# Attention's PSUM: four single slots chosen by an estimate in place of two rings of two, and the key load placed ahead of the maxima rows' loads

## The chip, the cores and the metric

The kernel runs on one core of one Trainium2 chip. The metric is the device time of one execution in microseconds (us). Before the change the median of 3 runs is 1422.26 us (1418.68 to 1423.93).

## The reference

For 8 batches of 8 heads, 1152 keys and 64 dimensions, neighbouring pairs of query rows are averaged to 576 queries, and softmax attention is computed with its row maxima subtracted. The result, as x of 576 x 512 for each batch, goes through a second part.

```
q_pool = q.reshape(B, H, S // 2, 2, D).mean(axis=3)
scores = scale * q_pool @ k^T;  scores -= max(scores);  attn = exp(scores)
x      = (attn / sum(attn)) @ v              # then heads side by side: 576 x 512
theta  = x @ w_theta;  y = w_tok_r @ (x cos theta) + w_tok_i @ (x sin theta)
u      = x + y;        out = u + max(u @ w_ch, 0)
```

## The kernel before, in words

The work is in two stages with a PSUM pool each. The first, attention, is what the change touches; the second (theta, token mixing, channel product) is left alone.

**The tiling of attention.** Heads go in 32 pairs i = 0 .. 31, the two heads side by side in the 128 partitions of the matrix array. A pair has two halves of 288 queries (u = 0, 1) with nine key tiles each (kt = 0 .. 8). For each (u, kt):

- `escore` (lines 354 to 374) makes the scores in eight matmuls, two heads by four terms: high by high part, high by low, low by high, and last the row of negated maxima (`nmr`, line 371). They go to a double bank `pe` of PSUM, from which ScalarE takes the exponential into a tile `pc` (line 374).
- `ssum` (376 to 383) adds the `pc` tiles on GpSimd to `ss`, 4.5 steps later.

The maxima of a pair are found one to two pairs earlier. `maxpass` (296 to 315) makes twelve rough score products, two matmuls each into a double bank `pm` (305), and VectorE reduces each (312). `max_tail` does the remaining 64 queries (`px`, `py`, lines 322 and 328), `max_nm` joins them (337), `max_row` transposes the result into `pmt` (342) and ScalarE copies it to `mT` (344). `load_max` then spreads `mT` into the row `nmr` with four DMAs (351, 352).

At two places of each pair a `burst` (456 to 466) comes between the score tiles.

- With u = 0: `prep_t` transposes queries and the last three key tiles of pair i + 2 into `pt` (265), which ScalarE copies to `hi` (281) and VectorE subtracts to `lo` (292); then `max_row` of pair i + 1; then `av`, 36 matmuls of `pc` by v into `pa` (392), copied out by ScalarE (399); then `norm_sum` of pair i - 1, twelve matmuls with ones (408), read by ScalarE (417). Before the change `norm_sum` writes the second bank of the tile `pmt` that `max_row` took.
- With u = 1: `prep_t` transposes the first six key tiles of pair i + 3, then `max_tail` of pair i + 2, then `av`.

So between two runs of `av` there is a **stretch** of nine score products `pe` with six maxima products `pm` among them. The order is the same in both halves: pe pm pe pm pe pm pe pe pm pe pm pe pm pe pe, and then the burst's transposes into `pt`.

**The order of the work.** Nothing is scheduled by a planner. Each step has a position written by hand (`at(position, priority, step)`), in units of one score tile; pair i begins at 18 i. The list is sorted by position, and each engine takes its instructions in that order. So an instruction that waits holds up all that is behind it on its engine. In between, at nine positions per pair (`W_AT`), a generator `weights` does one step of narrowing and splitting a tile of the second stage's weights, on VectorE (lines 525 to 540), ScalarE and GpSimd; it also takes a double bank (`pwt`, line 585) ten times in all.

**PSUM before.** Attention owns all eight banks as four double banks, made by `bank2` (148). Two form the ring "e": `pe` and `pa` (for pair 0 also two thirds of `pm`). Two form the ring "m": `pm`, `pt`, `px`, `py`, `pmt`, `pwt`. In a ring of two a use waits until the readers of the use before last in that ring are done.

**The queue of loads.** SyncE issues all DMAs of this stage in order. The key tile `kn` has one buffer: the load of pair i + 3 (line 226, two DMAs) has to wait for the last transposes of pair i + 2's keys, in the burst with u = 0. `PLAN` puts that load at 36 - 43.2 = -7.2 relative to the next pair's start, behind `load_max` at -7.6.

Of the kernel before, what the change touches and what calls it, by code (L numbers as in the profile page):

```python
# [9 lines left out]
F32 = mybir.dt.float32  # L10
# [21 lines left out]
    "load_q": -44.55,  # L32
    "load_k": -43.2,
    "pool_q": -35.35,
# [12 lines left out]
BANKS = {}  # L47
PAIRS = {"e": 2, "m": 2}
BANKS2 = {"h": 1, "t": 1, "m": 4, "r": 2}
# [42 lines left out]
def pooled_attention_moe_kernel(  # L92
# [12 lines left out]
    P = 128  # L105
# [10 lines left out]
    NPAIR = B * NP  # L116
# [8 lines left out]
    psum = {}  # L125
# [18 lines left out]
    def bank(kind, name):  # L144
        pool, bufs = psum["now"]
        return pool.tile([P, 512], F32, tag=kind, name=name, bufs=bufs[kind])

    def bank2(kind, name):
        return psum["now"][0].tile([P, 2, 512], F32, tag=kind, name=name, bufs=PAIRS[kind])

# [37 lines left out]
    with ExitStack() as p1:  # L188
# [63 lines left out]
        def prep_t(i, g):  # L252
            st = state[i]
            kn = st["kn"]
            pt = st["pt", g] = bank2("m", f"pt{g}_{i}")
            if g == 0:
                srcs = [[kn[:, t] for t in range(3 * n, 3 * n + 3)] for n in range(2)]
            else:
                qp = st["qp"]
                srcs = [[qp[:, t] for t in range(5)], [qp[:, 5]] + [kn[:, t] for t in (6, 7, 8)]]  # L260
            for n in range(2):
                c = 0
                for src in srcs[n]:
                    R = src.shape[0]
                    nc.tensor.transpose(  # L265
                        out=pt[:, n, c : c + R],
                        in_=src.rearrange("p h d -> p (h d)"),
                        identity=ident[0:R, 0:R],
                    )
                    c += R  # L270
# [25 lines left out]
        def maxpass(i):  # L296
# [4 lines left out]
            for j in range(4):  # L301
                for g in range(3):
                    pm = bank2("em"[g % 2] if i == 0 else "m", f"pm{i}_{j}{g}")
                    for h, hs in enumerate(HEADS):
# [12 lines left out]
        def max_tail(i, pt):  # L317
            st = state[i]
            hi, tl, mx = st["hi"], st["tail"], st["mx"]
            pm = bank2("m", f"px{i}")  # L320
            for n, c, k, w in ((0, 0, 0, 4), (1, 0, 4, 2), (1, 2 * P, 6, 2)):
# [4 lines left out]
            if pt is None:  # L326
                pt = bank2("m", f"py{i}")
            nc.tensor.matmul(
# [10 lines left out]
        def max_row(i):  # L339
            st = state[i]  # L340
            px = bank2("m", f"pmt{i}")
            nc.tensor.transpose(out=px[0:KT, 0, 0:P], in_=st["nm"], identity=ident)
            mT = st["mT"] = sml.tile([KT, P], F32R, tag="mT", name=f"mT{i}")
            nc.scalar.copy(mT, px[0:KT, 0, 0:P])
            return px

# [38 lines left out]
        def av(i, u):  # L385
            st = state[i]
            if u == 0:
                st["xu"] = nrm.tile([P, 2, HALF], F32, tag="xu", name=f"xu{i}", bufs=3)
            pa = bank2("e", f"pa{i}_{u}")
            for kt in range(KT):  # L390
# [65 lines left out]
        def burst(i, u):  # L456
            if u == 0:
                if i + 2 < NPAIR:
                    prep_all(i + 2, 1)
                px = max_row(i + 1) if i + 1 < NPAIR else bank2("m", f"pmt{i}")  # L460
                av(i, u)
                if i > 0:
                    norm_sum(i - 1, px)
            else:
                tail_prep(i)
                av(i, u)
# [29 lines left out]
        def weights():  # L496
# [78 lines left out]
            def token(wv, kb, jt):  # L575
# [8 lines left out]
                yield  # L584
                pw2 = bank2("m", "pwt")
                pt = pw2[:, 0]
# [55 lines left out]
        NU = 2 * KT  # L642
        todo = []

        def at(pos, prio, fn, *args):
            todo.append((pos, prio, len(todo), fn, args))
# [37 lines left out]
        for i in range(NPAIR):  # L684
            plan(i)
        at(NU * NPAIR + 2, 9, lambda: norm_sum(NPAIR - 1, bank2("m", "pend")))
        pw = ExitStack()
# [303 lines left out]
```

## Time and profile before

| what | value |
|---|---|
| median of 3 runs | 1422.26 us (1418.68 to 1423.93) |
| span of the profiled execution, first to last instruction | 1414.8 us |
| median of the runs less that span | 7.5 us |
| PE matmul busy | 1352.8 us, 96% |
| VectorE (DVE) busy | 862.2 us, 61% |
| ScalarE (ACT) busy | 730.6 us, 52% |
| GpSimd (POOL) busy | 911.4 us, 64% |
| chain that ended last: PE, DVE, ACT, DMA | 67%, 15%, 10%, 3% |

The profiled execution's own time is known only as its span; launch and end around the instructions lie outside it, so the median of the runs stands 7.5 us above it. Matmuls are pipelined: one of 288 columns is recorded as 0.29 us long though the next one starts 0.07 us later. The busy share of PE therefore hides short waits, and starts of instructions tell more than durations. A name such as `PE pe L371` is engine, tile written and line; "x2" in a row joins two instructions in a line.

### The profile page before, as it was taken

The numbers are of one execution on the slowest core, as the hardware profiler recorded it, in microseconds if no ns is written. First come the engines' busy times: TensorE is split into PE (matmuls) and PEld (weight loads), VectorE is DVE, ScalarE is ACT, GpSimd is POOL, SyncE is SP. The second block draws the span as 40 slices with busy tenths as digits, with TensorE's granted clock in tenths as the row PEclk, the third lists the DMA queues.
The fourth block names the chain that finished last, engine by engine and source line by source line (L and its number), as shares of the span: only waits on it lengthen the run. The fifth ranks groups of instructions, "written<-read, shape, count | busy, mean of one in ns | idle before, by whom it ended". The sixth has DMA issues, their size and how long they took to land.

```text
span 1414.8 us, 29922 instructions
## 1 busy us (share of the span) xinstructions
PE 1352.8 (96%) x12178; PEld 1086.1 (77%) x12178; DVE 862.2 (61%) x1143; ACT 730.6 (52%) x1250; POOL 911.4 (64%) x672
## 2 busy tenths in 40 slices
PE   5999999999999999999999999999999999999998
PEld 4667676766676767767776766688999999999998
DVE  5866676777577767766687666355362553536442
ACT  2556465655555655556565655465444544445431
POOL 2789888978798889889898888834232413232210
PEclk7999999999999999999999999999999999999999
DMA  5224343434342443324343421231111211111111
GB/s 127 74 75 126 85 111 84 119 85 116 86 125 69 108 122 106 94 83 125 84 111 86 119 80 51 79 122 38 35 38 34 60 50 34 38 35 44 28 31 38
DMA packets 130906, 111.66 MB, mean 79 GB/s; under 512 B 95040, under 2 KB 95424, under 8 KB 130768
## 3 DMA queue, kind: packets, MB, share of 16 engines
q1 hardware_dynamic: 130592, 109.28, 28.0%
q8 instruction: 96, 1.57, 0.5%
q0 software_dynamic: 176, 0.46, 0.1%
q14 instruction: 42, 0.34, 0.1%
HBM read 88.29 MB, written 21.27 MB: 77 GB/s over the span
## 4 chain that ended last, share of the span: by engine, by line
PE 67%; DVE 15%; ACT 10%; DMA 3%; issue 3%; POOL 1%; SPq 0%; ACTq 0%; POOLq 0%; DVEq 0%
PE pa L392 16%; PE pe L371 16%; PE py L821 11%; PE pth L743 7%; PE pr L860 5%; DVE mx L312 5%; ACT pc L374 4%; PE pm L305 3%; PE pt L265 3%; PE pmt L408 2%; DMA kn<-in_k_dram 2%; DVE wf L532 1%; PE pxn L731 1%; DVE ws L530 1%; DVE lo L292 1%
## 5 line engine op out<-in xcount | busy, mean ns | idle before, releaser
L383 POOL TENSOR_TENSOR ss<-ss,pc 128x576 f32<-128x576 f32 x384 | 558.1, 1453 | 98.2 <-ACT pc L374 75.9
L312 DVE TENSOR_REDUCE mx<-pm 128x2 f32<-128x768 f32 x384 | 343.9, 950 | 134.8 <-PE pm L305 134.4
L374 ACT ACTIVATE pc<-pe 128x576 f32<-128x576 f32 x576 | 371.2, 652 | 102.2 <-PE pe L371 84.2
L392 PE MATMUL pa<-pc,vn 128*64 128x288 f32 x2304 | 293.5, 409 | 0.3 <-ACT pc L374 0.3
L794 POOL TENSOR_TENSOR Z<-ab,Z 128x512 fp32r<-128x512 f32 x40 | 52.2, 1305 | 306.0 <-ACT Z L790 277.8
L392 PEld LDWEIGHTS pa<-pc,vn 128*64 128x64 f32 x2304 | 159.7, 137 | 110.7 <-ACT pc L374 4.8
L821 PE MATMUL py<-wtk,Z 128*128 128x288 f32 x1728 | 241.7, 297 | 0.0
L821 PEld LDWEIGHTS py<-wtk,Z 128*128 128x128 f32 x1728 | 233.2, 189 | 1.3
L371 PE MATMUL pe<-hi 64*128 64x288 f32 x1152 | 203.1, 349 | 14.9 <-ACT pc L374 6.5
L371 PEld LDWEIGHTS pe<-hi 64*128 64x128 f32 x1152 | 108.3, 184 | 92.9 <-ACT pc L374 57.9
L371 PE MATMUL pe<-hi,lo 64*128 64x288 f32 x1152 | 170.8, 293 | 0.0
L371 PE MATMUL pe<-lo,hi 64*128 64x288 f32 x1152 | 170.8, 293 | 0.0
L371 PE MATMUL pe<-nmr,oner 64*128 64x288 f32 x1152 | 169.5, 290 | 0.0
L305 PE MATMUL pm<-hi 64*128 64x384 f32 x768 | 138.1, 359 | 14.6 <-DVE mx L312 8.6
L371 PEld LDWEIGHTS pe<-lo,hi 64*128 64x128 f32 x1152 | 109.8, 187 | 0.0
L371 PEld LDWEIGHTS pe<-hi,lo 64*128 64x128 f32 x1152 | 109.1, 186 | 0.0
L371 PEld LDWEIGHTS pe<-nmr,oner 64*128 64x128 f32 x1152 | 109.0, 185 | 0.0
L292 DVE TENSOR_TENSOR lo<-pt,hi 128x768 fp32r<-128x768 f32 x64 | 67.6, 1057 | 66.9 <-ACT hi L281 66.9
L860 PEld LDWEIGHTS pr<-us,wch 128*128 128x128 f32 x768 | 104.5, 188 | 2.0
L860 PE MATMUL pr<-us,wch 128*128 128x288 f32 x768 | 105.8, 295 | 0.0
L281 ACT CAST hi<-pt 128x768 fp32r<-128x768 f32 x64 | 56.2, 878 | 91.5 <-DVE mx L332 74.3
L383 POOL TENSOR_TENSOR ss<-pc,pc 128x576 f32<-128x576 f32 x64 | 93.8, 1466 | 3.0 <-ACT pc L374 3.0
(105 smaller groups left out, 1652.7 us busy)
## 6 DMA issues: line engine op xcount, KB each, us to landing
qn<-in_q_dram SPq DMA_DIRECT2D x32, 576.0 KB
kn<-in_k_dram SPq DMA_DIRECT2D x64, 288.0 KB
vn<-in_v_dram SPq DMA_DIRECT2D x32, 576.0 KB
dn<-ro SPq DMA_DIRECT2D x64, 144.0 KB
xd<-xu SPq DMA_DIRECT2D x32, 288.0 KB
xT<-xd SPq DMA_DIRECT2D x8, 1152.0 KB
out_dram<-on SPq DMA_DIRECT2D x23, 192.0 KB
out_dram<-on SPq DMA_DIRECT2D x23, 128.0 KB
```

Of the source, the lines that this page charges most:

```text
L281: nc.scalar.copy(hi, src)
L292: nc.vector.tensor_tensor(lo, src, hi.bitcast(F32), ALU.subtract)
L305: nc.tensor.matmul(pm[:, h, 0:W], hi[hs, Q0 + j * P : Q0 + (j + 1) * P], hi[hs, K0[3 * g] : K0[3 * g] + W], start=True, stop=True,)
L312: nc.vector.tensor_reduce(mx[:, j : j + 5 : 4, g : g + 1], pm[:, :, 0:W], AX.X, ALU.max)
L371: nc.tensor.matmul(pe[:, h, 0:HALF], w[hs], x[hs], start=(n == 0), stop=(n == 3))
L374: nc.scalar.activation(pcs[u, kt], pe[:, :, 0:HALF], AF.Exp, scale=SC)
L383: nc.gpsimd.tensor_tensor(st["ss", u], first, st["pc"][u, kt], ALU.add)
L392: nc.tensor.matmul(pa[hs, 0, 0:HALF], st["vn"][:, h, kt, :], st["pc"][u, kt][:, h, :], start=(kt == 0), stop=(kt == KT - 1),)
L743: nc.tensor.matmul(th, xs[c][:, j * P : (j + 1) * P], ws[:, c], start=(n == 0), stop=(n == 11))
L794: engine("zlo", b).tensor_tensor(Z[1], t, Z[0].bitcast(F32), ALU.subtract)
L821: nc.tensor.matmul(st["py", c, u][:, 0:HALF], Z[zi][:, c * P : (c + 1) * P], wtk[wi][:, kw, u * HALF : (u + 1) * HALF], start=(i == 0 and ...
L860: nc.tensor.matmul(pr[u][:, 0:HALF], wch[wi][:, c, e * P : (e + 1) * P], st["us", ui][:, c, u * HALF : (u + 1) * HALF], start=(n == 0), st ...
```

## The change

`bank2` no longer takes the next of a ring. There are four slots b0 to b3, each one double bank with one buffer. While the program is written, three clocks are kept: PE ("p"), ScalarE ("a") and VectorE ("d"), and for each slot the time at which it is estimated to be free. A use takes the slot with the least such time. By the table `HOLD` (work on PE, engines that read, time of the reading) its end is estimated and becomes the slot's new time. The choice is fixed in the program: at run time a use waits for the readers of the slot's last use, whichever engine they are on. The table knows the uses of double banks alone; VectorE's and ScalarE's other work is not in it.

Two more things change. `norm_sum` gets a double bank of its own ("ns") and no longer shares `pmt`. And `load_k` moves from -43.2 to -43.62, which is 36 - 43.62 = -7.62 relative to the next pair's start: its two DMAs now stand ahead of `load_max`'s four at -7.6 in SyncE's queue.

```diff
 PLAN = {
     "load_q": -44.55,
-    "load_k": -43.2,
+    "load_k": -43.62,
...
-PAIRS = {"e": 2, "m": 2}
+SLOTS = 4
+HOLD = {
+    "e": (0.54, "a", 0.6),
+    "pm": (0.17, "d", 0.95),
+    "pt": (0.75, "ad", 2.1),
+    "px": (0.6, "d", 1.55),
+    "pa": (4.4, "a", 0.4),
+    "mt": (0.2, "a", 0.3),
+    "ns": (1.0, "a", 0.5),
+    "pw": (0.75, "ad", 1.9),
+}
...
+    clock = {"p": 0.0, "a": 0.0, "d": 0.0}
+    slots = [0.0] * SLOTS
+
     def bank2(kind, name):
-        return psum["now"][0].tile([P, 2, 512], F32, tag=kind, name=name, bufs=PAIRS[kind])
+        n = min(range(SLOTS), key=lambda k: slots[k])
+        work, engines, after = HOLD[kind]
+        clock["p"] = max(clock["p"], slots[n]) + work
+        end = max([clock["p"] + 0.3] + [clock[e] for e in engines]) + after
+        for e in engines:
+            clock[e] = end
+        slots[n] = end + 0.1
+        return psum["now"][0].tile([P, 2, 512], F32, tag=f"b{n}", name=name, bufs=1)
...
-            pt = st["pt", g] = bank2("m", f"pt{g}_{i}")
+            pt = st["pt", g] = bank2("pt", f"pt{g}_{i}")
...
-                    pm = bank2("em"[g % 2] if i == 0 else "m", f"pm{i}_{j}{g}")
+                    pm = bank2("pm", f"pm{i}_{j}{g}")
...
-            pm = bank2("m", f"px{i}")
+            pm = bank2("px", f"px{i}")
...
-                pt = bank2("m", f"py{i}")
+                pt = bank2("px", f"py{i}")
...
-            px = bank2("m", f"pmt{i}")
+            px = bank2("mt", f"pmt{i}")
...
-            return px
...
-            pa = bank2("e", f"pa{i}_{u}")
+            pa = bank2("pa", f"pa{i}_{u}")
...
-                px = max_row(i + 1) if i + 1 < NPAIR else bank2("m", f"pmt{i}")
+                if i + 1 < NPAIR:
+                    max_row(i + 1)
                 av(i, u)
                 if i > 0:
-                    norm_sum(i - 1, px)
+                    norm_sum(i - 1, bank2("ns", f"pns{i}"))
...
-                pw2 = bank2("m", "pwt")
+                pw2 = bank2("pw", "pwt")
...
-        at(NU * NPAIR + 2, 9, lambda: norm_sum(NPAIR - 1, bank2("m", "pend")))
+        at(NU * NPAIR + 2, 9, lambda: norm_sum(NPAIR - 1, bank2("ns", "pend")))
```

## Rows read from the trace of the kernel before

**Rows 1.** Busy time of each engine in three stages of attention: the start, the steady part and the end. Columns: stretch, its length, then busy us (and instructions) of PE, PE's weight loads, DVE, ACT and POOL, PE's granted clock as a share of 2.4 GHz, DMA share, GB/s.

```profile
20.00:47.00 27.00, 20.90 (x160) 17.18 (x160) 20.15 (x25) 11.02 (x18) 12.65 (x10) 0.73 0.31 86
47.00:885.00 838.00, 808.17 (x8357) 585.47 (x8353) 588.41 (x693) 477.51 (x825) 719.26 (x523) 1.00 0.36 97
885.00:919.00 34.00, 30.61 (x319) 21.24 (x317) 12.89 (x13) 16.98 (x30) 29.25 (x21) 1.00 0.24 76
```

**Rows 2.** The view of waits: who waited for whom, us in total, number of times, longest.

```profile
PEld pe L371 <- ACT pc L374: 57.9, 196, 1.2
PE pe L371 <- ACT pc L374: 6.5, 20, 0.9
PEld pm L305 <- DVE mx L312: 15.9, 25, 1.6
PE pm L305 <- DVE mx L312: 8.6, 21, 1.3
PE pt L265 <- DMA kn<-in_k_dram: 12.4, 8, 7.7
PE pmt L408 <- ACT mT L344: 3.8, 6, 1.6
```

**Rows 3.** The timeline of PE in one stretch of nine score products: start, duration, instruction, idle time before it and what ended it. The first row is the first matmul of the stretch, the last the burst's first transpose.

```profile
732.65 0.40 PE L371 MATMUL pe<-hi 64*128 64x288 f32 x2
733.28 0.34 PE L305 MATMUL pm<-hi 64*128 64x384 f32 x2
733.45 0.30 PE L371 MATMUL pe<-hi 64*128 64x288 f32 x2
733.98 0.34 PE L305 MATMUL pm<-hi 64*128 64x384 f32 x2
734.19 0.40 PE L371 MATMUL pe<-hi 64*128 64x288 f32 x2
...
739.72 0.71 PE L265 MATMUL pt<-ident,qp 96*128 96x96 f32 x6
```

**Rows 4.** The timelines of ACT and of DVE in the same stretch.

```profile
733.49 1.35 ACT L374 ACTIVATE pc<-pe 128x576 f32<-128x576 f32 x2 [0.32 <-PE pe L371]
735.09 1.35 ACT L374 ACTIVATE pc<-pe 128x576 f32<-128x576 f32 x2 [0.25 <-PE pe L371]
...
733.66 2.69 DVE L312 TENSOR_REDUCE mx<-pm 128x2 f32<-128x768 f32 x3 [1.24 <-PE pm L305]
```

**Rows 5.** The timeline of PE at the bounds of two other stretches that lost little, the first and the last of 26 that took 7.06 to 7.20 us.

```profile
92.00 0.40 PE L371 MATMUL pe<-hi 64*128 64x288 f32 x2
...
99.09 0.71 PE L265 MATMUL pt<-ident,qp 96*128 96x96 f32 x6
...
871.26 0.40 PE L371 MATMUL pe<-hi 64*128 64x288 f32 x2
...
878.38 0.28 PE L342 MATMUL pmt<-ident,nm 128*9 128x128 f32 x1
```

**Rows 6.** The timelines of DVE and of PE in stretches with a weights step among the reductions: in the first of 16 such second halves a step of line 528 and the maxima product that then waited, then the bounds of that stretch, and those of the last of the 16.

```profile
148.42 1.48 DVE L528 TENSOR_SCALAR wf<-raw 128x576 uint32<-128x576 uint32 x1
...
146.53 0.40 PE L371 MATMUL pe<-hi 64*128 64x288 f32 x2
...
150.82 0.44 PE L305 MATMUL pm<-hi 64*128 64x384 f32 x2 [0.26 <-DVE mx L312]
...
154.19 0.71 PE L265 MATMUL pt<-ident,qp 96*128 96x96 f32 x6
...
816.76 0.40 PE L371 MATMUL pe<-hi 64*128 64x288 f32 x2
...
824.72 0.71 PE L265 MATMUL pt<-ident,qp 96*128 96x96 f32 x6
```

**Rows 7.** One key load in the steady part: PE's last transposes of the keys before it, SyncE's issue of the maxima rows and of the keys, and PE's first transposes of those keys.

```profile
294.18 0.49 PE L265 MATMUL pt<-ident,kn 128*128 128x128 f32 x3
...
299.49 0.66 SPq L351 DMA_DIRECT2D nmr<-mT  x1
...
302.77 1.58 SPq L226 DMA_DIRECT2D kn<-in_k_dram  x2
...
308.50 0.84 PE L265 MATMUL pt<-ident,kn 128*128 128x128 f32 x6 [0.65 <-DMA kn<-in_k_dram]
```

**Rows 8.** The start: PE's last transposes of pair 1's keys, the last of the four maxima loads of pair 0, PE's first two matmuls that use them, and DVE's reductions ahead of the first `av`.

```profile
27.47 0.85 PE L265 MATMUL pt<-ident,kn 128*128 128x128 f32 x3
...
27.92 0.53 SPq L352 DMA_DIRECT2D nmr<-mT  x1
...
30.57 0.44 PE L371 MATMUL pe<-nmr,oner 64*128 64x288 f32 x2
31.54 0.44 PE L371 MATMUL pe<-nmr,oner 64*128 64x288 f32 x2
...
39.84 6.14 DVE L312 TENSOR_REDUCE mx<-pm 128x2 f32<-128x768 f32 x7
```

**Rows 9.** The end of attention: GpSimd's last sums, and PE's last `norm_sum`, which needs them.

```profile
898.44 10.66 POOL L383 TENSOR_TENSOR ss<-ss,pc 128x576 f32<-128x576 f32 x6 [2.25 <-ACT pc L374]
...
911.23 8.87 POOL L383 TENSOR_TENSOR ss<-ss,pc 128x576 f32<-128x576 f32 x6 [0.50 <-ACT pc L374]
...
919.59 1.01 PE L408 MATMUL pend<-ss,ones 128*32 128x288 f32 x5
```

## The prediction, made blind

> **What bounds the kernel now.** I read the stages first. In the steady part of attention PE counts as busy for 808 of 838 us, GpSimd for 719, VectorE for 588, ScalarE for 478 [rows 1]. So PE's stream of instructions sets the time, and GpSimd is the next in line. The share of busy time hides waits, so the view of waits comes next. PE's largest is for the exponential before a score product can go into its double bank: 57.9 + 6.5 = 64.4 us. Then maxima products wait 24.5 us for VectorE's reductions; transposes wait 12.4 us for keys, 7.7 of them at the very start, so 4.7 later; and `norm_sum` waits 3.8 us for the copy `mT` out of the tile it shares [rows 2].
>
> Then one stretch of nine pe and six pm shows how the 64.4 us arise. Take starts: a pe that did not wait takes 0.53 us (733.45 to 733.98), one that waited 0.63 (732.65 to 733.28), a pm 0.17 [rows 3]. Without waits the stretch would be 9 x 0.53 + 6 x 0.17 = 5.8 us; it takes 739.72 - 732.65 = 7.07. An exponential is 0.65 long, and two in a row start 0.70 apart (1.35 less 0.65). The first ends at 734.14 and the third pe starts at 734.19: it waited for that double bank [rows 3, 4]. In the ring of two, one slot's round is pe, exponential, 0.05 to release, next pe: from 733.49 to 735.09, 1.60 for two score products [rows 4]. That is 0.8 each, where ScalarE could do 0.70 and PE 0.53 to 0.7.
>
> **The slots, walked through.** I went through the diff's arithmetic in the order of the code. In the steady part the choice repeats; in a second half it reads (use: slot, whose last use was): pe1 b2, a pe long done; pm1 b0, pt; pe2 b1, px; pm2 b3, pa; pe3 b2, pe1; pm3 b0, pm1; pe4 b1, pe2; pe5 b3, pm2; pm4 b2, pe3; pe6 b1, pe4; pm5 b0, pm3; pe7 b3, pe5; pm6 b2, pm4; pe8 b1, pe6; pe9 b0, pm5. The first half has the same shape. So of the nine pe, five still wait for the exponential of the pe two before, as now; pe5 and pe9 now wait for a reduction, and pm4 for an exponential. What is gained lies at pe5 and pe9.
>
> **Stretches (the main term).** I step through it with the rows' durations: exponential 0.84 after the first pe's start, 0.90 after a pe that waited, 0.79 after another (estimate: 0.11 less), never under 0.70 after the one before; reduction 0.39 after the pm's start, 0.95 long, 0.87 from one to the next (2.69 less 0.95, halved); release 0.05 [rows 3, 4]. For the rings this gives pe starts at 0, 0.81, 1.54, 2.35, 3.14, 3.95, 4.75, 5.56, 6.35 and an end at 7.06, where 7.07 is measured. For the slots: 0, 0.81, 1.54, 2.35, 2.89 (pm2's reduction ends at 2.84), 3.84, 4.65, 5.45, 6.08 (pm5's ends at 5.82), end 6.69. A clean stretch gains 0.37 us, not the 1.2 that its waits add up to.
>
> Not every stretch is clean. Of 60, 26 take 7.06 to 7.20 us [rows 5]. In 16 second halves a weights step of 1 us and more stands on VectorE behind the first reduction, and PE waits for the later ones: 7.66 in the first, 7.96 in the last [rows 6]. With a step of 1.45 us there, my steps give 7.70 for the rings, and 7.89 for the slots: pe5 now waits for the delayed second reduction (4.29), where in the ring it ran ahead and only pm4 waited. That is 0.19 lost. The two break even at a step of 0.6 us. Eight first halves have a shorter step one place later, worth about +0.1 each; four hold a `pwt` and I give them 0; six wait for keys and are otherwise clean. Sum: (26 + 6) x 0.37 + 8 x 0.1 - 16 x 0.19 = 11.8 + 0.8 - 3.0 = **9.6 us** less. Bounds: 60 x 0.37 = 22 less; all disturbed, 60 x 0.19 = 11 more. I take the mixture, since it is counted from the stretches themselves.
>
> Against the number: the Trainium skill, page "Perfetto Trace Analysis", section "Matmuls", says that independent matmul groups should rotate through different PSUM banks, so that emptying one overlaps the next group. By it the waits for exponentials would go as a whole, 64.4 us and not 9.6. No run here shows that yet; the trace agrees only that such waits exist.
>
> **Keys.** Today the issue of the keys stands behind four maxima loads that start at 299.49, though the old keys' last transposes ended at 294.67; it comes at 302.77, and PE's transposes start at 308.50 after a wait for them [rows 7]. Moved ahead, the two DMAs can go at about 294.7 and need 308.50 - 304.35 = 4.1 us after their issue: there by 300.4, some 8 us before their use. The queue's four maxima loads come after them; they wait for `mT` until 299.49 anyway and are used only by the next pair's first pe, behind the whole stretch, so the 1.6 us of issue cost nothing. v's load and the sums' behind them come no later. I take the 4.7 us and 0.1 for each of seven restarts: **5 us** less; bounds 3 and 6.
>
> **`norm_sum`'s own slot.** Its 3.8 us of waiting for `mT` go [rows 2]. The exponentials behind `mT` on ScalarE stay late, so **3.5** less; bounds 0 and 3.8. Its slot b0 was freed by pe9's exponential, long before `av` ends, so no new wait there.
>
> **The start (a cost).** For pair 0 the keys' load (of pair 2) now stands ahead of `load_max`, and must wait for pair 1's transposes, which end at 28.32. Two DMAs (1.6) and four loads (0.66 each) then end at about 32.5 instead of 28.45. Today the first use is at 30.57, 2.1 after that [rows 8]; so it moves to at most 34.6, by 3 to 4 us, and with it the first exponential and all behind on PE and ScalarE. VectorE sets the pace after it: reductions run without a gap from 39.84 to 45.98 [rows 8], but it had some 2.5 us of idle time between 30.4 and 39.84 that is made up. So **2 us** more; bounds 0 and 7, the upper if PE's clock (1.2 GHz here, a pe takes 0.97 [rows 1, 8]) rises later by as much again.
>
> **The end.** The last three stretches hold pe alone, with three or four slots in turn. PE gains some 2 us in each, but GpSimd's sums run from 898.44 to 920.10 with 0.50 us of idle time, after 2.25 before, and the last `norm_sum` needs them [rows 9]. So at most 2.75: I take **2.7** less.
>
> **Nothing else.** PE's, ScalarE's and VectorE's instructions are the same in number. GpSimd's 719 us fit in a stage of some 820 [rows 1]. The second stage depends on attention's end alone.
>
> **Sum.** -9.6 - 5 - 3.5 + 2 - 2.7 = -18.8. On the profiled span 1414.8 - 18.8 = 1396.0; the runs' median stands 7.5 above the span, so **1403.5 us**, 1.3% less. A measurement here can tell about 0.5%, or 7 us, from no change.
>
> **Rivals.**
>
> 1. *VectorE's lateness reaches the score products everywhere: slower.* The place is pe5 and pe9 behind reductions; the estimate knows nothing of weights steps, `norm_out` or reciprocals on VectorE. It decides from 0.6 us of foreign work per stretch on. For it: 24.5 us of waiting for reductions today [rows 2], 16 stretches as in [rows 6]. Against: 26 clean ones. Price: two such delays per stretch, 60 x 0.38 = +23; keys, `norm_sum` and end back -11, start +2: **1436**.
> 2. *The stretches gain nothing*, because five of nine pe wait as before and the exponentials of a stretch end only 0.2 us earlier (7.70 against 7.90 for the ninth). Left: -5 - 3.5 + 2 - 2.7 = -9: **1413**; with the start at its bound, 1418.
> 3. *Every stretch gains the clean 0.37*, since the delays are taken up by slack that I don't see: -22 - 6 - 3.8 + 0 - 2.75: **1388**. A whole removal of the 64.4 us would give 1349; ScalarE's pace of 0.70 speaks against it, 1 in 100, inside this rival.
> 4. *PE's clock.* It is 1.00 of 2.4 GHz through the whole steady part, with PE waiting 0.1 to 0.3 us at every second pe [rows 1, 3]; a cycle of other waits might lose it in places. At 1.2 GHz a pe costs 0.97 for 0.53 [rows 3, 8], 9 x 0.44 = 4 us per stretch; six stretches are +24: **1428**. The Trainium skill, page "TensorE: Matmul & The Clock Gate", section "A second HAM failure mode: psum-queue depth-cycling", tells of a kernel whose cycling through PSUM made PE idle briefly and its clock go to and fro. By that rule this change could bring it; the trace of before disagrees, since its waits left the clock whole.
>
> **How the numbers follow.** My forecast 0.47 (1394 to 1411, faster); rival 1 0.13 (slower); rival 2 0.22, of which 0.07 is still beyond 0.5% and 0.15 is no change; rival 3 0.14 (faster); rival 4 0.04, half no change, half slower. Faster 0.47 + 0.14 + 0.07 = 0.68; same 0.15 + 0.02 = 0.17; slower 0.13 + 0.02 = 0.15. The range 1386 to 1424 leaves out rival 1, half of 4 and the lower part of 3, together about 0.2. For the cases that gain alone it would be 1386 to 1413.
>
> **What would show it.** Right: a clean stretch of 6.7 us with the fifth pe 0.53 after the fourth; disturbed second halves of 7.8 to 8.1, and there `pe` waiting for `mx`; no steady wait of `pt` for keys; none of `norm_sum` for `mT`; the first `nmr` matmul at about 34; the waits of pe for exponentials down by a third or so. Wrong: clean stretches still at 7.07, or a new large wait of `pe` for `mx` in most of them, or `pc` waiting for `ss`.

## The result, and the profile after

The changed kernel takes 1395.97 us (median of 4 runs, 1395.23 to 1396.66) against 1420.47 us of the kernel before (4 runs): ratio 0.9832, 95% interval 0.9811 to 0.9852, so 1.7% less. The forecast was 1403.5 us in a range of 1386 to 1424, and faster. The profiled span went from 1414.8 to 1393.2 us, 21.6 less; 18.8 less was the sum. The other part of the miss is the distance from span to median: 7.5 us for the kernel before, 2.8 after. I carried the first over as if it were fixed, and as if it were launch and end. It is not: every execution of the changed kernel and of the runs below took 1.7 to 2.1 us more than its own span. So the profiled execution of before, with its span of 1414.8, took some 1416.8 us, about as long as the fastest of its four runs (1416.92), and the rest of the 7.5 is the difference between that execution and the median. With 2.0 for 7.5 the same sum gives 1398.0.

Beside the runs below the kernel before took 1417.05 to 1418.72 us (medians of 8 to 19 runs). Against these the changed kernel stands at 0.984 to 0.985, so its gain is 1.5 to 1.7%.

The stages after, to be read against [rows 1] (stretch, length, busy us and instructions of PE, weight loads, DVE, ACT, POOL, granted clock as a share of 2.4 GHz, DMA share, GB/s):

```profile
49.00:856.00 807.00, 788.90 (x8291) 582.50 (x8287) 585.86 (x693) 470.37 (x822) 715.09 (x519) 1.00 0.38 100
856.00:891.00 35.00, 34.79 (x382) 24.71 (x382) 16.38 (x13) 17.40 (x35) 33.39 (x22) 1.00 0.27 82
```

The steady part is shorter with nearly the same work in it, so waits went; PE's clock stayed whole. At the end GpSimd is now busy for 33.4 of 35 us. The waits of the changed kernel, against [rows 2]:

```profile
PEld pe L390 <- ACT pc L393: 34.0, 134, 0.7
...
PEld pe L390 <- DVE mx L332: 10.1, 13, 1.4
...
PE pt L285 <- DMA kn<-in_k_dram: 7.8, 1, 7.8
...
PE pe L390 <- DVE mx L332: 7.3, 10, 1.2
```

PEld is the load of weights that goes ahead of each matmul, and its waits and those of PE must not be added: they are the same waits, seen twice. At 745.21 us the weight load waits 1.04 us, and the matmul's 0.80, shown further down, lie inside that:

```profile
745.21 0.18 PEld L390 LDWEIGHTS pe<-hi 64*128 64x128 f32 x2 [1.04 <-DVE mx L332]
```

So score products wait 34.0 us for exponentials (57.9 before) and, which is new, 10.1 us for VectorE's reductions. The forecast's 64.4 and 24.5, and the 17.4 in an expectation below, each count such waits twice. Keys are waited for once, at the start. A wait of `norm_sum` for `mT` no longer stands among the large ones.

PE in the stretch that answers to [rows 3] (same pair and half):

```profile
713.36 0.40 PE L390 MATMUL pe<-hi 64*128 64x288 f32 x2
...
715.71 0.30 PE L390 MATMUL pe<-hi 64*128 64x288 f32 x2
...
716.25 0.40 PE L390 MATMUL pe<-hi 64*128 64x288 f32 x2
...
720.08 0.39 PE L285 MATMUL pt<-ident,qp 96*128 96x96 f32 x2
```

The fifth pe starts at 2.89 (716.25 less 713.36), 0.54 behind the fourth, and the stretch takes 6.72 us where 7.07 was [rows 3]. The forecast said 2.89 and 6.69.

The answer to [rows 6]: a stretch with a step on VectorE and the first reduction on time, on DVE and PE.

```profile
742.80 1.49 DVE L548 TENSOR_SCALAR wf<-raw 128x576 uint32<-128x576 uint32 x1
...
740.91 0.40 PE L390 MATMUL pe<-hi 64*128 64x288 f32 x2
...
743.61 0.40 PE L390 MATMUL pe<-hi 64*128 64x288 f32 x2 [0.18 <-ACT pc L393]
...
745.21 0.40 PE L390 MATMUL pe<-hi 64*128 64x288 f32 x2 [0.80 <-DVE mx L332]
...
748.82 0.55 PE L285 MATMUL pt<-ident,qp 96*128 96x96 f32 x4
```

Here the fifth pe waits 0.80 us for the second reduction, which stands behind the step; it starts at 4.30 (4.29 was stepped through), and the stretch takes 7.91 us (7.89). And the answer to [rows 7], PE's last transposes of the old keys and SyncE's queue:

```profile
287.95 0.49 PE L285 MATMUL pt<-ident,kn 128*128 128x128 f32 x3
...
288.48 1.36 SPq L246 DMA_DIRECT2D kn<-in_k_dram  x2
293.97 0.68 SPq L370 DMA_DIRECT2D nmr<-mT  x1
```

The keys are issued right behind those transposes, 5.5 us ahead of the first maxima load.

All of the span's 21.6 us, by the forecast's terms (stretch by stretch in the two traces; waits for keys lie inside the stretches, so the seven with such waits are one line; of the nine with a `pwt`, two have it just ahead of the stretch):

| term | forecast | measured |
|---|---|---|
| clean stretches (26 forecast; 24 so sorted) | -9.6 | -7.4 |
| first halves that wait for keys (6; 7) | -7.2 | -8.0 |
| other first halves (8; 7) | -0.8 | -2.5 |
| disturbed second halves (16; 13) | +3.0 | +1.4 |
| stretches with a `pwt` (4; 9) | 0 | -2.1 |
| bursts | 0 | -2.5 |
| `norm_sum` | -3.5 | -3.3 |
| start, to the first `av` | +2 | +1.96 |
| end, from 856 us on | -2.7 | +0.7 |
| sum | -18.8 | -21.6 |

The start, against [rows 8]: issue of the keys, the last of the four maxima loads behind them, the first maxima row on PE, and VectorE's long run of reductions.

```profile
29.09 1.31 SPq L246 DMA_DIRECT2D kn<-in_k_dram  x2
...
32.85 0.53 SPq L371 DMA_DIRECT2D nmr<-mT  x1
...
33.74 0.94 PE L390 MATMUL pe<-nmr,oner 64*128 64x288 f32 x2 [2.22 <-DMA nmr<-mT]
...
41.88 6.14 DVE L332 TENSOR_REDUCE mx<-pm 128x2 f32<-128x768 f32 x7
```

PE's first maxima row comes 3.2 us later (30.57 before), VectorE's run 2.04 later (39.84 before): the idle time in between took up the rest, as the forecast said.

The end, against [rows 9], on POOL and PE:

```profile
872.42 11.42 POOL L402 TENSOR_TENSOR ss<-ss,pc 128x576 f32<-128x576 f32 x7
...
885.89 9.54 POOL L402 TENSOR_TENSOR ss<-ss,pc 128x576 f32<-128x576 f32 x6
...
895.48 0.70 PE L427 MATMUL pend<-ss,ones 128*32 128x288 f32 x3 [3.63 <-POOL ss L402]
...
898.29 1.11 PE L751 MATMUL pxn<-ident,xT 128*128 128x128 f32 x4 [0.66 <-ACT sm L436]
899.05 3.03 PE L763 MATMUL pth<-wth,xh 128*128 128x512 f32 x8
...
903.20 2.10 PE L763 MATMUL pth<-wth,xh 128*128 128x512 f32 x8
```

PE gained 6.1 us in the last three stretches and then waited 3.63 us for GpSimd's sums. The granted clock around that wait:

```profile
891.00:896.00 5.00, 1.36 (x13) 0.37 (x13) 0.98 (x1) 0.40 (x1) 4.76 (x5) 0.82 0.17 61
896.00:901.00 5.00, 4.34 (x23) 2.68 (x16) 0.04 (x1) 1.09 (x2) 1.44 (x1) 0.50 0.81 253
901.00:906.00 5.00, 5.00 (x25) 4.10 (x24) 2.05 (x4) 1.16 (x2) 0.00 (x0) 0.99 0.25 70
```

At 0.50 of 2.4 GHz, that is 1.2, the first eight `pth` take 3.03 us instead of 2.10. From the last `av`'s start to the end of the span it was 1414.8 - 915.07 = 499.7 us and is 1393.2 - 886.66 = 506.5.

### The profile page after: what moved, and what is told of

The parts are those of the page before. It is cut to its first block, busy times and chain, and to the rows that moved or that the text cites. A ratio compares the mean times of both kernels' runs of the same rounds, so it can differ in the third digit from the quotient of the medians.

```text
span 1393.2 us, 29952 instructions
## 1 busy us (share of the span) xinstructions
PE 1342.4 (96%) x12178; PEld 1088.3 (78%) x12178; DVE 864.6 (62%) x1143; ACT 724.0 (52%) x1250; POOL 914.4 (66%) x672
## 4 chain that ended last, share of the span: by engine, by line
PE 72%; DVE 15%; ACT 7%; DMA 3%; issue 2%; POOL 1%; SPq 0%; ACTq 0%; POOLq 0%; DVEq 0%
PE pe L390 18%; PE pa L411 17%; PE py L841 11%; PE pth L763 7%; PE pr L880 6%; DVE mx L332 5%; PE pt L285 4%; PE pm L325 3%; PE pns L427 2%; ACT pc L393 2%; PE pxn L751 1%; DVE r L785 1%; DVE r L786 1%; PE po L903 1%; DVE mx L351 1%
## 5 line engine op out<-in xcount | busy, mean ns | idle before, releaser
L332 DVE TENSOR_REDUCE mx<-pm 128x2 f32<-128x768 f32 x384 | 347.5, 951 | 125.6 <-PE pm L325 124.0
L393 ACT ACTIVATE pc<-pe 128x576 f32<-128x576 f32 x576 | 364.8, 652 | 98.2 <-PE pe L390 85.6
```

The source lines that it names most:

```text
L332: nc.vector.tensor_reduce(mx[:, j : j + 5 : 4, g : g + 1], pm[:, :, 0:W], AX.X, ALU.max)
L393: nc.scalar.activation(pcs[u, kt], pe[:, :, 0:HALF], AF.Exp, scale=SC)
```

## The experiments

Each was timed beside the kernel before; a ratio is to that kernel. "First `av`" is its start (46.5 before, 48.5 after), "stretches" the sum over all against before (-24.6 for the full change).

**The key load alone.**

```diff
 # kernel before
-    "load_k": -43.2,
+    "load_k": -43.62,
```

> The kernel before with the key load's move alone. Theory (the terms add up): the 4.7 us of waiting for keys in the steady part and their seven restarts go, the start costs 2 us as in the trace of after (first av 48.5 for 46.5): about 3 us less than before, some 1417 us, with the first use of the maxima row near 33.7. Rival (the key load is what the whole change gained by): 10 us less or more, 1411 or below.

Measured: 1416.08 us, ratio 0.9992 (0.9980 to 1.0004). The stretches gain 5.9 us and no wait for keys is left but the first, as expected, but the first `av` starts at 50.4, 3.9 later, and not 2. Alone the move is worth nothing that can be told.

**Slots and `norm_sum`'s bank, without the key load.**

```diff
 # changed kernel
-    "load_k": -43.62,
+    "load_k": -43.2,
```

> The changed kernel with the key load back behind the maxima rows. Theory: the slots and norm_sum's own bank carry most of the 24 us; keys are waited for again, in more bursts than before since PE comes to them sooner, 6 to 9 us, and the start is 2 us cheaper: 1400 to 1403 us, 4 to 7 above the changed kernel. Rival: the two parts do not touch, then 1399. Rival (slots gain nothing without the keys): 1412 or more.

Measured: 1408.14 us, ratio 0.9929 (0.9909 to 0.9948), outside all three expectations. The first `av` starts at 44.4, 2.1 earlier than before: the slots help the start, so the +1.96 of the full change is about +3.9 and -2.1. The stretches gain only 7.9, and 6.1 of that is in the last three: the first sixty gain 1.8, where the full change has 18.5. The wait for keys in this kernel:

```profile
PE pt L285 <- DMA kn<-in_k_dram: 17.4, 10, 7.7
```

Less the first, that is 9.7 us where it was 4.7 [rows 2]: a PE that runs ahead comes to the late keys sooner. In nineteen of 60 stretches the time differs by more than 0.12 from the full change, 16.6 us in all, most of it in first halves that now take 7.3 to 8.7 where 6.8 is clean. The 5 us more of waiting for keys are a third of that; what makes the rest stays open. So the two parts are not additive: the key move is worth about 1 us alone, which can't be told from nothing, and 12 to 14 us with the slots (1405.9 - 1393.2 by the spans, 0.9929 - 0.9832 by the ratios).

**`norm_sum`'s own bank alone.**

```diff
 # kernel before
-                px = max_row(i + 1) if i + 1 < NPAIR else bank2("m", f"pmt{i}")
+                if i + 1 < NPAIR:
+                    max_row(i + 1)
...
-                    norm_sum(i - 1, px)
+                    norm_sum(i - 1, bank2("m", f"pns{i}"))
```

> The kernel before, with norm_sum in a double bank of its own from the ring m, rings kept. Theory: only the 3.3 us go by which av's end was followed late by norm_sum: 1417 us, stretches as before (7.07). Rival: the third use in a row of the ring m makes the next maxima product wait for the sums' reading by ScalarE, and the gain goes: 1420 or more.

Measured: 1419.44 us, ratio 1.0014 (0.9999 to 1.0029). Gone are the waits for `mT`; in the ring, in their place:

```profile
PEld pns L408 <- ACT tail L288: 5.7, 6, 2.3
```

The stretches lose 5.7 us, 4.3 of it in first halves, and the waits for keys grow from 12.4 to 14.2. That one more use in a ring of two shifts who follows whom, and so costs the rest, is argued and not shown. In the rings the bank of its own brings nothing.

**Four slots in plain turn.**

```diff
 # changed kernel
-        n = min(range(SLOTS), key=lambda k: slots[k])
+        n = int(clock["n"]) % SLOTS
+        clock["n"] = clock.get("n", 0) + 1
```

> The changed kernel, but slots taken in turn b0 b1 b2 b3 and not by the estimate. Stepped through with the rows' durations: a clean stretch 6.61 us (slots by estimate 6.69, rings of two 7.06), one with 1.45 us of weights work behind the first reduction 8.06 (7.89, 7.70). Theory (the pooling gains, the estimate hardly matters): 1394 to 1400 us. Rival (the estimate is the gain): at least a third of the stretches' gain is lost, 1403 or more.

Measured: 1399.83 us, ratio 0.9862 (0.9839 to 0.9886), at the upper end of the theory. Sharing four slots gives most of the gain. Its clean stretches are even better, 6.62 against 6.71; what it loses is in stretches with other work on VectorE:

```profile
PEld pe L391 <- DVE mx L333: 31.0, 69, 2.0
...
PE pe L391 <- DVE mx L333: 17.2, 23, 1.7
```

So 31.0 us of waiting for reductions, against 10.1 with the estimate. Eight first halves that take 6.8 to 6.9 with the estimate take 7.2 here, in most of them with a weights step of 0.7 us behind the second reduction, and two that take 7.0 take 8.72 and 10.28. In the last of these PE waits 1.73 us, and its granted clock is 0.50 from 113.0 to 116.4 us.

**A worse estimate.**

```diff
 # changed kernel, HOLD
-    "pm": (0.17, "d", 0.95),
+    "pm": (0.17, "d", 1.3),
```

> The changed kernel with the table's time of VectorE for a pm raised from 0.95 to 1.3, nothing else: the same four slots, another choice. Theory (which slot a use takes matters, not only that the four are shared): stepped through with the rows, a clean stretch takes 7.26 instead of 6.69 and a disturbed one 7.53 instead of 7.89; some 30 clean ones lose 0.57 and 16 disturbed ones gain 0.36, about 11 us more, 1403 to 1410 us. Rival (any sharing of four slots does it, as the run with the slots in plain turn nearly did with 1400): 1394 to 1400 us.

Measured: 1422.12 us, ratio 1.0041 (1.0024 to 1.0057): slower than the kernel before. One number in the table costs 26 us, and the rival (any sharing does it) falls. The same stretch as above:

```profile
736.52 0.40 PE L390 MATMUL pe<-hi 64*128 64x288 f32 x2
...
739.05 0.29 PE L390 MATMUL pe<-hi 64*128 64x288 f32 x2
...
739.68 0.40 PE L390 MATMUL pe<-hi 64*128 64x288 f32 x2
...
743.78 0.47 PE L285 MATMUL pt<-ident,qp 96*128 96x96 f32 x3
```

The fifth pe is back at 3.16, where the rings had it stepped through at 3.14, and the stretch takes 7.26 us, as stepped through beforehand. Clean second halves mostly take 7.23 to 7.28; eight with a step on VectorE take 7.47 to 7.52, stepped through as 7.53. So for second halves in which the step stands where I had put it, the step-through from the rows' durations holds to 0.08 us for three choices (rings, slots, worse slots). The total is more than the 11 expected: the stretches lose 19.6, since few were left that the other choice helps, and the bursts 6 more, which I had not stepped through.

**A weights step moved ahead of the reductions**, in the changed kernel and in the one before.

```diff
-W_AT = (9.45, 9.5, 9.85, 10.5, 12.75, 18.0, 18.6, 19.25, 20.45)
+W_AT = (9.45, 9.5, 9.85, 10.5, 12.75, 18.0, 18.6, 19.25, 19.3)
```

(`W_FIRST` likewise.)

> The changed kernel with the ninth weights step of each pair moved from position 20.45, where it stands on VectorE behind the first reductions of a second half, to 19.3, before the half's av ends; the steps are the same in number. Theory (the slots couple a late reduction to the score products of the next slots): the 29 second halves lose most of their excess of 18.5 us over the clean 6.7, some 12 us come back, so about 1384 us, and the waits of pe for mx fall from 17.4 us to under 7. Rival (the excess is ScalarE's or the burst's, not VectorE's): no change, 1393 to 1399, because the delayed copies of the transposes take up what the stretches gain.

> The kernel before with the same weights step moved from 20.45 to 19.3. Theory (in the rings the late reductions delay only pm, and pm then the score products behind it): the excess of the second halves is 11.0 us here and not 18.5, so some 8 us are to be had at most, about 1412 us against 1419; the gap between this kernel and the changed one with the same move is then wider than between the two without it, about 28 us and not 23. Rival (ring and slots suffer alike from VectorE): both gain the same, the gap stays at 23 to 24 us.

Measured: 1401.92 us, ratio 0.9891 (0.9876 to 0.9906), and 1421.88 us, ratio 1.0028 (1.0016 to 1.0039). Both are slower than without the move, by 6 and by 4 us, so both theories missed. In the changed kernel eight second halves gain 0.16 to 1.2 us, as the theory had it, but six lose 1 to 2.3: at 19.3 the step stands right behind that of 19.25, and the two together delay the first reduction. In one of the worst, on DVE and PE:

```profile
201.84 1.38 DVE L552 TENSOR_SCALAR wf<-ws 128x576 uint32<-128x576 uint32 x1
203.25 1.85 DVE L556 SCALAR_TENSOR_TENSOR wf<-raw,wf 128x576 uint32<-128x576 uint32 x1
...
205.15 2.62 DVE L332 TENSOR_REDUCE mx<-pm 128x2 f32<-128x768 f32 x3
...
206.09 0.44 PE L325 MATMUL pm<-hi 64*128 64x384 f32 x2 [2.36 <-DVE mx L332]
...
207.91 0.52 PE L325 MATMUL pm<-hi 64*128 64x384 f32 x2
```

PE waits 2.36 us, and its clock is lost on top: 0.72 on the mean of 207 to 213 us.

```profile
207.00:213.00 6.00, 6.00 (x60) 5.62 (x58) 4.19 (x6) 3.85 (x7) 2.72 (x3) 0.72 0.51 147
```

In the last of the six PE waits as long, and the clock stays whole:

```profile
808.52 0.45 PE L325 MATMUL pm<-hi 64*128 64x384 f32 x2 [2.36 <-DVE mx L332]
...
809.00:815.00 6.00, 6.00 (x70) 4.79 (x68) 4.49 (x7) 4.56 (x7) 3.86 (x3) 1.00 0.55 150
```

The three of the six with a fall of the clock lose 2.1 to 2.3 us, the three without 1.0 to 1.2.

The kernel before takes 10.57 us in the half shown first with the move, the changed one 10.61, and the gap between the two kernels is 1.4% with the move and 1.7% without, not wider. Over all stretches the move costs 6.5 us with the rings and 7.2 with the slots. So rings and slots suffer about alike from a long delay of the reductions. That the slots suffer more is not borne out; but the move made delays and took none away, so what the theories price, their removal, was not tested.

**The step behind the last reduction.**

```diff
 # changed kernel
-W_AT = (9.45, 9.5, 9.85, 10.5, 12.75, 18.0, 18.6, 19.25, 20.45)
+W_AT = (9.4, 9.45, 9.5, 9.85, 10.5, 12.75, 18.0, 18.6, 19.25)
```

> The changed kernel with the weights step of position 20.45 moved to 9.4 of the next pair, behind the last reduction of the second half instead of behind the first one; as many steps as before. Theory (a VectorE step ahead of a stretch's reductions costs what the moved one cost in the run that put it at 19.3, and is free where no reduction stands behind it): no second half loses as there, the mixed stretches of the second halves fall from 220 us to some 208 to 212, the excess that is left being that of the stretches with a pwt and of the step at 19.25; 1383 to 1388 us. Rival (four steps in a row now delay nm and the lo of the next burst): pmt waits for nm and pt's slot comes free late, what the stretches gain the bursts lose, 1393 to 1400 us.

Measured: 1392.97 us, ratio 0.9828 (0.9813 to 0.9842), whose interval overlaps the changed kernel's; its span is 1.2 us shorter. From pair 1 on no step stands between the reductions of a second half any more, yet these stretches take 217.8 us in all (220.3 in the changed kernel, 208 to 212 expected). Now other steps fall on 19.25: in ten second halves the first reduction starts 1.8 to 2.5 us after the first pe instead of 1.0, and the stretch takes 7.4 to 8.1. The rival's place was wrong too: the bursts do not lose (72.5 against 72.2). The delay moved along a chain of steps that must all go somewhere ahead of VectorE's reductions. What a better spacing of all nine would give was not tried.

**The end: the last sums on VectorE.**

```diff
 # changed kernel, ssum
-            nc.gpsimd.tensor_tensor(st["ss", u], first, st["pc"][u, kt], ALU.add)
+            eng = nc.vector if i == NPAIR - 1 and u == 1 else nc.gpsimd
+            eng.tensor_tensor(st["ss", u], first, st["pc"][u, kt], ALU.add)
```

> The changed kernel with the sums of the last half of the last pair on VectorE instead of GpSimd. Theory (the last stretches gained 6 us on PE and gave them back, since the last norm_sum waits for GpSimd's sums and PE's clock falls during that wait): PE no longer waits 3.63 us for ss ahead of the last norm_sum, the granted clock stays at 1.00 into the second stage, 4 to 7 us less, about 1390 us. Rival (the end is bound by ScalarE's exponentials and the reading of the sums, the wait for GpSimd only comes last by little): under 2 us, 1394 to 1397.

Measured: 1392.6 us, ratio 0.9822 (0.9807 to 0.9837), whose interval overlaps the changed kernel's; the rows decide. PE and DVE at the end:

```profile
889.00 5.07 DVE L403 TENSOR_TENSOR ss<-ss,pc 128x576 f32<-128x576 f32 x6
...
894.12 0.44 PE L428 MATMUL pend<-ss,ones 128*32 128x288 f32 x3 [0.25 <-DVE ss L403]
...
896.37 2.10 PE L764 MATMUL pth<-wth,xh 128*128 128x512 f32 x8
```

The wait is 0.25 instead of 3.63 us, the first `pth` run takes 2.10 instead of 3.03, and from the last `av`'s start to the end of the span it is 502.3 us instead of 506.5: 4.2 less, as the theory had it. Up to the second run of `pth` it is 5.6 less (10.9 us instead of 16.5), of which the second stage loses 1.4 again. The last `av` itself starts 2.0 later than in the changed kernel, by 0.6 at the start and 1.6 at a wait near 370 us, told of below.

**The start: pair 2's key load as before.**

```diff
 # changed kernel
-            at(base + pl["load_k"], 5, load_k, i)
+            at(base + (pl["load_k"] if i != 2 else -43.2), 5, load_k, i)
```

> The changed kernel with the key load of pair 2 alone (issued during pair 0) kept behind the maxima rows' loads, as before the change; the later pairs keep the new order. Theory (the start paid 1.96 us because the first maxima rows stood behind a key load that waits for pair 1's transposes): the first av starts at about 46.5 instead of 48.5, and 2 us less come out at the end, 1394 us; in the first pairs the transposes may wait once for keys, at most 1 us. Rival (VectorE's reductions set the start, the loads only fill it): the first av stays at 48.5, no change, 1396.

Measured: 1391.73 us, ratio 0.9812 (0.9796 to 0.9828). The first `av` starts at 45.45, 3.05 earlier, and VectorE's long run of reductions ahead of it at 38.84 instead of 41.88. So the loads set when that run begins, and the rival falls. The last `av` starts only 1.94 earlier.

**Both ends.** The two diffs above together.

> The changed kernel with both edits to its ends: the last half's sums on VectorE, and pair 2's key load behind the maxima rows' loads. Theory (the two are independent): 4.2 us less behind the last av, as in the run with the sums alone, and 2 to 3 us less at the start, 1388 to 1390 us. Rival (what the start gains is lost before the end, since both runs lost 1.3 to 1.6 us at one place near 370 us): 1391 to 1393 us.

Measured: 1390.33 us, ratio 0.9805 (0.9788 to 0.9822). The rest from the last `av` on is 503.3 us, the first `av` starts at 45.3, but the last starts at 886.68 as in the changed kernel (886.66): the start's 3.2 us were lost on the way, as the rival said, though the time lies just under its range. The place, on DVE:

```profile
371.90 0.46 DVE L546 TENSOR_SCALAR raw<-raw 128x576 uint32<-128x576 uint32 x1 [7.09 <-DMA raw<-in_moe_w_tok_i_dram]
372.27 1.15 DVE L312 TENSOR_TENSOR lo<-pt,hi 128x960 fp32r<-128x960 f32 x1
```

VectorE waits 7.09 us for a weight tile (5.4 in the changed kernel), the `lo` of the transposes stands behind that wait, and PE then waits 2.54 us for a copy behind `lo`. Its granted clock is 0.50 from 375.4 to 378.8 us.

**Both ends, and the token-mixing fetches one weights step earlier.**

```diff
 # the run above, token()
-                yield
                 raw, ws = fetch([(dst, wv[t, ps]) for dst, t, ps in segments(jt)], SQ)
                 yield
+                yield
                 yield
```

> The run with both ends once more, and each fetch of a token-mixing weight tile issued one weights step earlier. Theory (what the start gained was lost near 370 us, where VectorE waits 7.1 us for such a fetch and the lo of the transposes, the copies, the exponentials and two stretches stand behind it): that wait goes or falls under 3 us, the av to score product gap of 8.23 us there returns to about 5.6 and the two stretches of 8.38 and 7.56 to about 6.8; up to 5 us less than the run with both ends, 1385 to 1388 us. Rival (the queue of loads or the buffer is what holds that fetch, so that an earlier place in the program changes nothing, or it holds up the maxima rows behind it): 1389 to 1392 us.

Measured: 1386.08 us (5 runs, 1384.46 to 1386.73), ratio 0.9767 (0.9748 to 0.9785), whose interval lies below the changed kernel's. The wait falls:

```profile
367.87 0.86 DVE L546 TENSOR_SCALAR raw<-raw 128x576 uint32<-128x576 uint32 x1 [2.95 <-DMA raw<-in_moe_w_tok_i_dram]
```

The gap there from `av` to the first pe is 5.62 instead of 8.23 us, the two stretches 7.07 and 7.28 instead of 8.38 and 7.56, PE's clock stays at 1.00, and the last `av` starts at 882.28, 4.4 earlier than in the run before it. This version beats both kernels.

## Why the prediction was right, and where it was not

**Stretches.** The main step held: a clean stretch gains 0.37, since five of nine pe still wait for an exponential and pe5 and pe9 go early. Measured 7.07 to 6.72 in the stretch shown, and 20 of the 24 clean ones gain 0.33 to 0.40. The run with the worse estimate shows the same steps for another choice of slots. So the wait for exponentials was never to be had as a whole: of 57.9 us 34.0 stay, and 10.1 come new from VectorE. Taken as the end of all such waits, the sentence on the Trainium skill's page "Perfetto Trace Analysis", section "Matmuls" (rotate through banks), would have given 1349 us. With four shared banks in plain turn or by the estimate the trace shows 18.8 and 34.0 us of such waits on the weight loads still there: the rule names the direction and not the size.

**Disturbed second halves.** Where the step is 1.45 long and the first reduction on time, two stretches went from 7.63 and 7.67 to 7.87 and 7.91, +0.24 for the +0.19 forecast. But they are a minority, and were one before: of the 16 that I counted, six had the first reduction on time and the step behind it. In six, the last one of [rows 6] among them, a step already stood ahead of the first reduction, and four hold a `pwt` or a copy of it. After the change, in six the first reduction starts 1.9 to 2.3 us after the first pe, where before it was 1.1 to 1.7, because the step ahead of it is later against a faster PE: they lose 0.2 to 0.7. In three the step shrank, and they gain 0.4 to 0.5: the last section tells why. I had taken the step's length and place as given; both depend on how far ahead PE is. The errors nearly cancel (+1.4 for +3.0).

**What I gave as nothing.** Stretches with a `pwt` and the bursts gained 2.1 and 2.5 us; I had stepped through neither, although transposes, `px` and `pwt` shared a ring of two as the maxima products did. The bursts' gain is all in six that follow a stretch with a `pwt`. The other first halves, which I gave 0.1 each, gained 0.06 to 0.54.

**Keys.** 5 us, near the 5.9 that the stretches gain in the run with the key load alone, but that was only half the truth: the price of late keys is not a constant. Over the stretches it is 6 us with the rings and 17 with the slots (24.6 less 7.9). I added the terms as if each part saw the kernel before.

**`norm_sum`.** -3.3 for -3.5, but in the rings its own bank gives nothing.

**The start.** +1.96 for +2. The forecast had both parts: loads that come 3 to 4 us later, and 2.5 us of VectorE's idle time that is made up. But it is the slots that make it up: behind VectorE's wait for the late products 2.2 us of idle time are left in the run with the key load alone, none in the changed kernel. The sum came out, the reason was missing. In the run with the last sums on VectorE, whose start is the same, the first `av` is at 49.1 for 48.5, so such a difference is known to some 0.6 us.

**The end: the step that failed.** The bound was right as far as it went: GpSimd's last sum ended 24.7 us earlier than before, against 22.3 for the beginning of these stretches, so 2.3 of the 2.75 allowed. What I left out is that a PE which gains 6.1 us against an engine that gains 2.3 must wait for the rest, and that after 3.63 us of idling it went on at 1.2 GHz. That costs 2.2 us more: from the end of the wait to the first `pxn`, from there to the first `pth` and from that to the second PE takes 2.81, 0.76 and 4.15 us, and 1.84, 0.41 and 3.23 in the run with the last sums on VectorE, where it hardly waits. Wait and clock together eat up the 6.1; some 0.9 us more are lost in the second stage, for a reason that stays open. The term came out at +0.7 where -2.7 was forecast.

**The sum.** -21.6 for -18.8 is closer than its terms. Against the forecast the lines of the table are off by +2.2, -0.8, -1.7, -1.6, -2.1, -2.5, +0.2, 0 and +3.4: that they nearly cancel is luck.

**Rivals.** VectorE's lateness everywhere (1436): the mechanism exists, 10.1 us of it, but in few stretches. Nothing gained in the stretches (1413): refuted by 20 of 24 clean ones. Every stretch gains (1388): some did not. The clock: 1.00 through the whole steady part, so the cycling that the Trainium skill's page "TensorE: Matmul & The Clock Gate" tells of did not come; in the stretches shown the clock is lost behind waits of 2.36 and 3.63 us, which a moved step and the change's own end make.

## What to carry to other kernels

Before pricing a wait, step through one period with the rows' durations, for the old and for the new assignment of buffers; it was good to 0.08 us here where the stretch was as the steps assume, and the waits of a stretch (1.2 us) said three times the 0.37 that came. Look first at what the other engines do in each stretch, since most of the disturbed ones were not as assumed. Do not add the waits of weight loads to those of their matmuls. Then ask of each part of a change what it is worth once the others are in: a load that was barely late becomes late when the engine in front of it gets faster, and an engine off the critical path that gains less than the bound becomes the wait at the next meeting point. An allocation by estimate is only as good as its table: one number of 0.95 raised to 1.3 turned 1.7% less into 0.4% more.

## What the runs showed of the hardware

The same instruction on VectorE took 1.48 us in one kernel and 0.45 in the other. In the kernel before it started 0.26 us after a GpSimd sum (the step itself stands in [rows 6]):

```profile
148.16 3.01 POOL L383 TENSOR_TENSOR ss<-ss,pc 128x576 f32<-128x576 f32 x2 [1.53 <-ACT pc L374]
```

After the change it started 0.13 us before the end of one GpSimd sum (146.24 and 1.43 long) and 0.21 us ahead of the next:

```profile
147.54 0.45 DVE L548 TENSOR_SCALAR wf<-raw 128x576 uint32<-128x576 uint32 x1
...
146.24 1.43 POOL L402 TENSOR_TENSOR ss<-pc,pc 128x576 f32<-128x576 f32 x1
147.75 3.02 POOL L402 TENSOR_TENSOR ss<-ss,pc 128x576 f32<-128x576 f32 x2
```

The two kernels run this step on such a tile twenty times in attention. Twice no GpSimd instruction was under way, and it took 0.45 us. In 17 of the other 18 it took 0.32 to 0.33 us more than was left of the GpSimd instruction that was under way, from 0.45 with 0.13 left to 1.70 with 1.37 left. The reductions, which read PSUM, took 0.95 in both kernels. This fits the Trainium skill's page "SBUF — State Buffer", section "SBUF: two separate sides": VectorE, in a two-port mode or with two inputs from SBUF, and GpSimd share a pair of ports that whichever starts first holds for its whole instruction. The rows show VectorE held up by GpSimd; the other direction, and whether this step runs in such a mode, no run here shows. So where in a GpSimd sum such a step begins is worth 1 us, and a change of order on PE shortened work on VectorE that nobody had touched.

PE's clock fell to 1.2 GHz after it had idled 3.63 us at the end and, in the run with the moved step, 2.36 us in a stretch, and full work went on at that level before it rose again, so these waits cost more than their length. But the length of a wait does not tell by itself whether the clock falls. It fell behind a wait of 1.73 us (plain turn, 112.70 us) and stayed at 1.00 behind one of 2.36 us in the run with the moved step, one of 2.40 us with the last sums on VectorE (377.49) and one of 2.52 us without the key load (619.97). Waits of pe of up to 1.2 us in the steady part of the changed kernel left it at 1.00.
